# How the second token chunk's normalized input gets from token order to feature order through device memory

## The chip, the core and the metric

The kernel runs on one core of a Trainium2 chip. The metric is the device time of one launch in microseconds (us), taken as the median of several runs. The trace comes from one profiled execution of the same program. Five engines work side by side, each through its own list of instructions in order, and wait for one another through semaphores: TensorE (PE in the profile, with PEld for its weight loads), VectorE (DVE), ScalarE (ACT), GpSimd (POOL) and SyncE (SP). SP computes nothing; it issues all of this kernel's transfers between device memory and the on-chip memory, in the order of its list.

## What is computed

The input is 2048 tokens of 512 features, all in float32. After a first layernorm there are two branches: sliding-window attention with 32 heads of 16 and a window of 256, and a channel MLP with 1792 hidden units. Their product is added to the input:

```python
xn = _layernorm(x)
s = attention(xn, wqkv) @ wo            # 32 heads, causal, window 256
y = _layernorm(xn)
h = gelu(y @ w1 + b1)                   # 512 -> 1792
g = silu(h @ w2 + b2)                   # 1792 -> 512
return x + s * g
```

## The kernel before

**Stages.** The first 430 us or so are the attention with its projections, and the weights being brought in. What follows is the MLP, chunk by chunk of 512 tokens (c = 0 to 3). In chunks 0 and 1 the loop over `i` takes the 14 hidden blocks of 128 units one by one. A float32 product is made of three passes of halves: each operand is split into a rounded "high" part and the rest, the "low" part. So a hidden block is 12 matmuls (`hidden`), then ACT applies gelu with the bias (`activate`), ACT writes the high part `gh`, DVE the low part `gl` (`split_g`), and 12 matmuls (`project`) add the block into the four accumulators `acc` (tokens by features). At the end of a chunk `end_chunk` multiplies the attention outputs `ohl` with `wo` (matmuls into `s`, 48 in all), applies silu to `acc`, multiplies, adds x and stores.

**Two layouts.** The layernorm needs tokens on the partitions, the hidden matmul needs features on the partitions. For chunk 1, `y_steps` normalizes four tiles of 128 tokens by 512 features in `mlp["y"]` while chunk 0 is in its loop (i = 3 and 4). Then `turn_y(1, range(4))` transposes each tile on DVE, in place, in blocks of 32 by 32, and SP writes each tile to the scratch tensor `z_d` in device memory, 256 KB a tile, in rows of 2 KB. At i = 5 `fetch_y(1, kt, ...)` reads it back for the four feature blocks kt = 0 to 3: four transfers a block, 16 in all, each of 32 partitions with 16 pieces of 32 numbers (128 bytes), which puts the 32 by 32 blocks in their places. So `mlp["yy"][1][kt]` holds features by tokens. Last, `split` copies the high part into `mlp["yy"][0][kt]` on ACT and subtracts on DVE, at i = 12 for kt 0, at 13 for kt 1 and at 14 for kt 2 and 3. Chunks 2 and 3 use the same two functions later on.

**Attention outputs.** In the same loop `load_o(0, g)` brings in, for g = 0 to 3, the attention output `or` (from `oT_d`) and the inverse row sums into the end of the tile `w` (from `rden_d`, each row repeated for 16 partitions). `rden_d` is written by SP at i = 5, after DVE has made the reciprocals `den`, and the four pairs of loads follow it on SP's queue, then the 16 transfers of `fetch_y`. DVE multiplies pair g at i = 9 + g, and `split_o` splits the product at i = 10 + g.

**What sets the order.** Every engine's instructions are kept in program order here. On DVE the multiplication of pair 0 stands just ahead of `gl` of hidden block 10; on ACT the copy of feature block kt stands between the `gh` of one hidden block and the gelu of the next. The tile `g_first`, which has the same place in memory (tag `wa`) as the `gated` tile of `end_chunk`, holds the two hidden blocks that are used first. SP's list goes on, behind the `fetch_y` of chunk 1, with the four loads of the next y tiles and the four loads of x for `end_chunk`.

Hidden blocks run in the order 2, 3, 0, 1, 4, 5, 6 to 13 in chunk 0 and 0 to 13 in chunk 1. In the profile nearly every instruction has line L43, that of a helper through which they are all recorded, so groups are told apart by their tiles' names.

Of the kernel before, what the change touches and what calls it, by code (L numbers as in the profile page):

```python
# [9 lines left out]
F32 = mybir.dt.float32  # L10
F32R = mybir.dt.float32r
I32 = mybir.dt.int32
AF = mybir.ActivationFunctionType
# [4 lines left out]
S, D, H, DH, WIN, F = 2048, 512, 32, 16, 256, 1792  # L18
P = 128
NCH = S // 512  # L20
# [30 lines left out]
def mixer_kernel(ctx, tc, x, wqk, wv, wo, w1, b1, w2, b2, out):  # L51


    nc = SimpleNamespace(**{name: Ordered(tc, name) for name in ("tensor", "vector", "scalar", "gpsimd", "sync")})

    const = ctx.enter_context(tc.tile_pool(name="const", bufs=1))
    bigp = ctx.enter_context(tc.tile_pool(name="bigp", bufs=1))
    t2 = ctx.enter_context(tc.tile_pool(name="t2", bufs=5))
    small = ctx.enter_context(tc.tile_pool(name="small", bufs=3))
    dram = ctx.enter_context(tc.tile_pool(name="dram", bufs=1, space=bass.MemoryType.DRAM))  # L60
# [16 lines left out]
    def load(pool, tag, src, name, shape=(P, 512)):  # L77
        t = pool.tile(list(shape), F32, tag=tag, name=name)
        nc.sync.dma_start(t, src)
        return t  # L80
# [102 lines left out]
    oT_d = dram.tile([4, 8, 32, S], F32, name="oT_d")  # L183
# [2 lines left out]
    w_d = {"w1": dram.tile([P, NF * 512], F32, name="w1_d"), "w2": dram.tile([P, NF * 512], F32, name="w2_d"),  # L186
           "wo": dram.tile([P, 4 * 512], F32, name="wo_d")}
    g_d = dram.tile([NF, P, 512], F32, name="g_d")
    z_d = dram.tile([NCH - 1, 4, P, 512], F32, name="z_d")
    mT_d = dram.tile([NQ, NCH, 32, P], F32, name="mT_d")  # L190


# [45 lines left out]
    b1s = const.tile([P, NF], F32, name="b1s")  # L238
# [346 lines left out]
    mlp = {}  # L585
# [54 lines left out]
    def y_steps(a, b):  # L640
        run(mlp["ln"][a:b])

    def hidden_mm(ps, f, k):
        kt, (a, b) = k // 3, PASSES[k % 3]
        nc.tensor.matmul(ps, w1_part(a, f)[:, P * kt: P * (kt + 1)], mlp["yy"][b][kt],
                         start=(k == 0), stop=(k == 3 * KT - 1))
# [49 lines left out]
    n, raw = raws["qk"]  # L696
# [176 lines left out]
    for f in range(6, NF, 2):  # L873
        t = gp.tile([P, 2, 512], F32, tag="ohl", name=f"hr_{f}", bufs=4)
# [9 lines left out]
    def load_y(c):  # L884
        return load_x(c, ((mlp["yp"], "y"),), "y")

    def turn_y(c, tiles):

        for i in tiles:
            y = mlp["y"][i]  # L890
            nc.vector.transpose(y, y)
            nc.sync.dma_start(z_d[c - 1, i], y)

    def fetch_y(c, kt, dst):

        for k in range(4):
            at = z_d[c - 1, 0, 0, 128 * kt + 32 * k: 128 * kt + 32 * k + 32]
            nc.sync.dma_start(dst[32 * k: 32 * k + 32].rearrange("p (t j) -> p t j", j=32),
                              bass.AP(tensor=at.tensor, offset=at.offset, ap=[[512, 32], [32 * 512, 16], [1, 32]]))

    def load_o(c, g):

        cols = slice(512 * c, 512 * (c + 1))
        pool, tag = (t2, "t2") if c else (mlp["yp"], "y")
        raw = load(pool, tag, oT_d[g, :, 0:DH, cols], f"or_{c}_{g}")
        rec = mlp["w2", g // 2][:, 512 * (14 + g % 2): 512 * (15 + g % 2)].bitcast(F32)
        nc.sync.dma_start(rec, bass.AP(tensor=rden_d.tensor, offset=rden_d.offset + 8 * g * S + 512 * c,
                                       ap=[[S, 8], [0, DH], [1, 512]]))
        return raw, rec

    def split_o(c, g, raw):
        ohl = gp.tile([P, 2, 512], F32R, tag="ohl", name=f"ohl_{c}_{g}", bufs=4)
# [6 lines left out]
    def open_accs(c):  # L919
        return [ps_mx.tile([P, 2, 512], F32, tag="mx", name=f"acc_{c}_{i}") for i in range(2)]  # L920

    def split_g(c, f, g, cast):
        gh = gp.tile([P, 512], F32R, tag="gh", name=f"gh_{c}_{f}")
        gl = gp.tile([P, 512], F32R, tag="gl", name=f"gl_{c}_{f}")
        split(gh, gl, g, cast)
        return gh, gl
# [154 lines left out]
    for c in range(2):  # L1081
        accs = open_accs(c)
        gs, os_, hs, wanted = {}, [], {}, []
        made = ready if c == 0 else {}

        def hidden(f):
            hs[f] = (ps_yt if c and f % 2 else ps_st).tile([P, 512], F32, tag="b", name=f"h_{c}_{f}")
            for k in range(3 * KT):
                hidden_mm(hs[f], f, k)

        def activate(f):
            if f in made and f in soon:
                gs[f] = made[f]
                return
            src = made[f] if f in made else hs.pop(f)
            g = src if f in made and f < 2 else t2.tile([P, 512], F32, tag="t2", name=f"g_{c}_{f}")
            nc.scalar.activation(g, src, AF.Gelu_apprx_tanh, bias=b1s[:, f: f + 1])
            gs[f] = split_g(c, f, g, nc.scalar.copy)

        order = [2, 3, 0, 1, 4, 5, *range(6, NF)] if c == 0 else [*range(NF)]  # L1100
        ahead = 2 + c
        for f in range(ahead if c else 0):
            hidden(f)
        o_from, o_late = (0, 0) if c else (7, 1)
        nc.sync.on = True
        for i in range(NF + 1):
            if i < NF:
                activate(order[i])
            if c and i in (1, 2, 6, 7):
                y_steps(6, 10)  # L1110
            if c and i >= 10 and i < 14:
                second_y(i - 10)
            if c and i == 14:
                kept["w"] = bigp.tile([P, 768], F32R, tag="wb1", name="wsh")
                combine_w(0)
            if c == 0:
                for kind, f in late_w[LATE[i]: LATE[i + 1]]:
                    settle(kind, f, nc.scalar.copy, nc.vector)
            if i >= 1:
                project(accs, [(order[i - 1], gs.pop(order[i - 1]))], order[0], order[-1])  # L1120
            if i + ahead < NF and order[i + ahead] not in made and order[i + ahead] > 1:
                hidden(order[i + ahead])
            if c == 0:
                if i == 3:
                    mlp["ln"] = layernorm(mlp["y"], "C1", True)
                    y_steps(0, 5)
                if i == 4:
                    y_steps(5, 10)
                    turn_y(1, range(4))
                if i in (4, 5):  # L1130
                    for j in (2 * i - 8, 2 * i - 7):
                        nc.vector.reciprocal(den[:, P * j: P * (j + 1)], den[:, P * j: P * (j + 1)])
                if i == 5:
                    nc.sync.dma_start(rden_d.rearrange("g a (c t) -> (g a c) t", c=NCH), den)
                    wanted += [load_o(0, g) for g in range(4)]
                    for kt in range(KT):
                        fetch_y(1, kt, mlp["yy"][1][kt].bitcast(F32))
                for kt in {12: (0,), 13: (1,), 14: (2, 3)}.get(i, ()):
                    split(mlp["yy"][0][kt], mlp["yy"][1][kt], mlp["yy"][1][kt].bitcast(F32))
            else:  # L1140
                steps2(i)
            k = i - o_from
            if 0 <= k - 2 - o_late < 4:
                os_.append(split_o(c, k - 2 - o_late, wanted[k - 2 - o_late][0]))
            if 0 <= k - 1 - o_late < 4:
                nc.vector.tensor_mul(wanted[k - 1 - o_late][0], *wanted[k - 1 - o_late])
            if c and 0 <= k < 4:
                wanted.append(load_o(c, k))
            if c == 0 and i == NF:
                mlp["y"] = load_y(2)  # L1150
            if c:
                if i in (2, 3, 7, 8):
                    turn_y(2 + i // 5, (0, 1) if i in (2, 7) else (2, 3))
                if i == 3:
                    mlp["y"] = load_y(3)
                    kept[0] = gated[:, 2:4]
                    kept[1] = bigp.tile([P, 2, 512], F32, tag="wb1", name="y2_21")
                    for kt in range(KT):
                        fetch_y(2, kt, kept[kt // 2][:, kt % 2])
                if i in (8, 9):  # L1160
                    for kt in (2 * i - 16, 2 * i - 15):
                        put("21" if kt > 1 else "11", kt % 2, kept[kt // 2][:, kt % 2])
                if i == 8:
                    fetch_second()
                if i == 12:
                    fetch_pair(0)
            if c and i in (0, 1, 5, 6):
                y_steps(5, 6)
        nc.sync.on = False
        if c == 0:  # L1170
            gated = bigp.tile([P, 4, 512], F32, tag="wa", name="gated")

        def between(i):
            if c == 1 and i in (1, 2):
                split_w(0, 2 * i - 2)
                split_w(0, 2 * i - 1)
        end_chunk(c, accs, os_, between)
        if c == 0:
            steps2(-1)
# [99 lines left out]
    for i in range(NF):  # L1279
# [9 lines left out]
        if 5 <= i < 9:  # L1289
            raw, rec = wanted  # L1290
            nc.vector.tensor_mul(raw, raw, rec)
        if 4 <= i < 8:
            wanted = load_o(3, i - 4)
# [34 lines left out]
```

## Time and profile before

| | us |
|---|---|
| median of 3 runs | 747.17 |
| lowest and highest run | 746.42 and 747.22 |
| the profiled execution's own time | 746.98 |
| its span, first to last instruction | 745.2 |
| PE busy in the span | 728.8 (98%) |
| DVE busy | 516.5 (69%) |
| ACT busy | 440.1 (59%) |
| POOL busy | 297.5 (40%) |

How to read what is quoted below: a row of the timeline has start, length, engine, line, operation, tile written and tiles read, shapes, how often, and in brackets the idle time before it and what ended it. A row of the chain of waits has start, length, who held the chain, and how many instructions. Times count from the start of the span. `SPq` is SP's queue. A busy PE is one that has matmuls in its pipeline.

### The profile page before, as it was taken

The numbers are of one execution on the slowest core, as the hardware profiler recorded it, in microseconds if no ns is written. First come the engines' busy times: TensorE is split into PE (matmuls) and PEld (weight loads), VectorE is DVE, ScalarE is ACT, GpSimd is POOL, SyncE is SP. The second block draws the span as 40 slices with busy tenths as digits, with TensorE's granted clock in tenths as the row PEclk, the third lists the DMA queues.
The fourth block names the chain that finished last, engine by engine and source line by source line (L and its number), as shares of the span: only waits on it lengthen the run. The fifth ranks groups of instructions, "written<-read, shape, count | busy, mean of one in ns | idle before, by whom it ended". The sixth has DMA issues, their size and how long they took to land.

```text
span 745.2 us, 18812 instructions
## 1 busy us (share of the span) xinstructions
PE 728.8 (98%) x7360; PEld 585.6 (79%) x7360; DVE 516.5 (69%) x790; ACT 440.1 (59%) x744; POOL 297.5 (40%) x644
## 2 busy tenths in 40 slices
PE   8999999999999999999999999999999999999997
PEld 7886777777778887777776688788888888888886
DVE  6886777877766678887773567656658755676643
ACT  7757767867667676778877756443544734442001
POOL 7413757757666555767867700020102000001102
PEclk9999999999999999999999999999999999999999
DMA  8633355757555624646735385745453322253611
GB/s 289 192 71 77 86 137 149 210 151 194 142 133 153 154 71 149 163 129 165 201 103 161 92 286 201 198 143 194 110 108 113 96 88 74 69 181 117 214 55 56
DMA packets 84025, 105.71 MB, mean 142 GB/s; under 512 B 36640, under 2 KB 36896, under 8 KB 83936
## 3 DMA queue, kind: packets, MB, share of 16 engines
q1 hardware_dynamic: 83936, 104.50, 49.5%
q8 instruction: 58, 0.95, 0.5%
q14 instruction: 31, 0.25, 0.1%
HBM read 54.53 MB, written 32.77 MB: 117 GB/s over the span
## 4 chain that ended last, share of the span: by engine, by line
PE 86%; ACT 5%; DVE 3%; DMA 2%; issue 1%; POOL 1%; SPq 1%; DVEq 0%; ACTq 0%; POOLq 0%
PE fb L43 19%; PE acc L43 17%; PE zo L43 12%; PE stb L43 9%; PE p L43 9%; PE s L43 6%; PE h L43 6%; PE xy L43 5%; ACT pt L43 4%; PE pv L43 3%; POOL pt L43 1%; DVE xy L43 1%; SPq L43 1%; DMA w<-rden_d 1%; DMA xnT<-z_d 1%
## 5 line engine op out<-in xcount | busy, mean ns | idle before, releaser
L43 POOL TENSOR_SCALAR_AFFINE_SELECT pt<-pt 128x256 f32<-128x256 f32 x480 | 192.9, 425 | 133.7 <-ACT pt L43 131.7
L43 ACT ACTIVATE pt<-stb 128x768 f32<-128x768 f32 (+1 forms) x244 | 188.5, 773 | 62.4 <-PE stb L43 55.1
L43 DVE TENSOR_REDUCE mt<-xy 128x4 f32<-128x1024 f32 (+1 forms) x128 | 152.6, 1192 | 4.4
L43 DVE COPY_PREDICATED xy<-upper,zo 128x512 f32<-128x512 int32 x112 | 77.8, 695 | 70.6 <-PE xy L43 63.1
L43 POOL TENSOR_TENSOR xo<-xo,gated 128x512 f32<-128x512 f32 x15 | 19.9, 1330 | 236.9 <-DVE gated L43 195.5
L43 PE MATMUL fb<-xnT,wqb 64*128 64x512 f32 (+1 forms) x684 | 104.6, 397 | 0.2
L43 PE MATMUL zo<-pt,vt 128*17 128x128 f32 x2880 | 103.7, 275 | 0.3 <-POOL pt L43 0.3
L43 PE MATMUL stb<-qk 64*128 64x384 f32 (+1 forms) x488 | 97.1, 393 | 6.2 <-ACT pt L43 3.9
L43 PE MATMUL acc<-w,gh 128*128 128x512 f32 x320 | 98.6, 389 | 0.4 <-ACT gh L43 0.4
L43 PEld LDWEIGHTS stb<-qk 64*128 64x128 f32 x488 | 45.8, 183 | 51.5 <-ACT pt L43 46.3
L43 PEld LDWEIGHTS zo<-pt,vt 128*17 128x17 f32 x2880 | 67.5, 97 | 15.6 <-issue 6.3
L43 PEld LDWEIGHTS fb<-xnT,wqb 64*128 64x128 f32 (+1 forms) x684 | 64.7, 185 | 11.0 <-DVE pjr L43 1.4
L43 PEld LDWEIGHTS acc<-w,gh 128*128 128x128 f32 x320 | 60.0, 188 | 13.1 <-ACT gh L43 0.8
L43 PE MATMUL acc<-w,gl 128*128 128x512 f32 x160 | 62.3, 390 | 1.0 <-DVE gl L43 1.0
L43 PE MATMUL xy<-qk 64*128 64x256 f32 (+2 forms) x536 | 58.4, 291 | 0.2
L43 PEld LDWEIGHTS xy<-qk 64*128 64x128 f32 x536 | 46.6, 185 | 6.6 <-issue 3.1
L43 ACT COPY oraw<-zo 128x128 f32<-128x128 f32 x128 | 34.0, 266 | 29.4 <-PE zo L43 28.7
L43 PE MATMUL s<-wos,ohl 128*128 128x512 f32 (+1 forms) x204 | 44.3, 376 | 0.0
L43 ACT ACTIVATE gated<-acc 128x512 f32<-128x512 f32 x16 | 8.7, 596 | 59.3 <-DVE acc L43 59.3
L43 PEld LDWEIGHTS s<-wos,ohl 128*128 128x128 f32 x204 | 36.8, 188 | 7.1
L43 PEld LDWEIGHTS zo<-qk 64*128 64x128 f32 x448 | 38.5, 185 | 4.6 <-issue 1.4
L43 ACT COPY p<-p 128x512 f32<-128x512 f32 x21 | 12.3, 585 | 48.9 <-PE p L43 41.2
(191 smaller groups left out, 1233.8 us busy)
## 6 DMA issues: line engine op xcount, KB each, us to landing
qk<-sh SPq DMA_DIRECT2D x128, 128.0 KB
qk<-pjr SPq DMA_DIRECT2D x64, 128.0 KB
oT_d<-oraw SPq DMA_DIRECT2D x32, 256.0 KB
w_d<-in_w_dram SPq DMA_DIRECT2D x14, 512.0 KB
x<-in_x_dram SPq DMA_DIRECT2D x16, 256.0 KB
or<-oT_d SPq DMA_DIRECT2D x16, 256.0 KB
w<-rden_d SPq DMA_DIRECT2D x16, 256.0 KB
xo<-in_x_dram SPq DMA_DIRECT2D x16, 256.0 KB
```

What stands on the lines that cost most here:

```text
L43: r = issue(*args, **kwargs)
```

## The change

Chunk 1's y takes another way through memory, and some steps around it move.

- DVE transposes the four y tiles out of place into one tile `whole` (tag `wa`), so that the four token tiles' blocks of 32 lie next to one another: 128 numbers, 512 bytes, for each feature block of 32.
- SP writes `whole` to a new scratch tensor `zt_d` (features by tokens) in four transfers of 32 partitions by 16 pieces of 512 bytes, instead of four transfers in rows of 2 KB.
- SP reads each feature block back in one load of 128 rows of 2 KB, four in all, instead of 16 transfers of 128-byte pieces.
- The token columns come back in another order (32-token blocks of the four tiles interleaved). The 14 gelu instructions of chunk 1 write them back in order, through an output access pattern with runs of 32 numbers.
- `load_o` is cut in two. For chunk 0 the four `or` loads now stand ahead of the write of `rden_d`, and the four loads of the inverse sums behind the four loads of y.
- The split of feature block 0 moves from i = 12 to i = 9.
- `z_d` has one part less; chunks 2 and 3 use it as before.

```diff
-    z_d = dram.tile([NCH - 1, 4, P, 512], F32, name="z_d")
+    z_d = dram.tile([2, 4, P, 512], F32, name="z_d")
+    zt_d = dram.tile([S // 4, 512], F32, name="zt_d")
...
-            nc.sync.dma_start(z_d[c - 1, i], y)
+            nc.sync.dma_start(z_d[c - 2, i], y)
...
-    def load_o(c, g):
-
-        cols = slice(512 * c, 512 * (c + 1))
+    def load_raw(c, g):
+
         pool, tag = (t2, "t2") if c else (mlp["yp"], "y")
-        raw = load(pool, tag, oT_d[g, :, 0:DH, cols], f"or_{c}_{g}")
+        return load(pool, tag, oT_d[g, :, 0:DH, 512 * c: 512 * (c + 1)], f"or_{c}_{g}")
+
+    def load_rec(c, g):
+
         rec = mlp["w2", g // 2][:, 512 * (14 + g % 2): 512 * (15 + g % 2)].bitcast(F32)
         nc.sync.dma_start(rec, bass.AP(tensor=rden_d.tensor, offset=rden_d.offset + 8 * g * S + 512 * c,
                                        ap=[[S, 8], [0, DH], [1, 512]]))
-        return raw, rec
+        return rec
+
+    def load_o(c, g):
+        return load_raw(c, g), load_rec(c, g)
...
-            nc.scalar.activation(g, src, AF.Gelu_apprx_tanh, bias=b1s[:, f: f + 1])
+            to = g
+            if c:
+                src = src.rearrange("p (a i t) -> p a i t", a=4, i=4)
+                to = g.rearrange("p (i a t) -> p a i t", a=4, i=4)
+            nc.scalar.activation(to, src, AF.Gelu_apprx_tanh, bias=b1s[:, f: f + 1])
...
                 if i == 4:
                     y_steps(5, 10)
-                    turn_y(1, range(4))
+                    whole = bigp.tile([P, 16, 4, 32], F32, tag="wa", name="y_1")
+                    for j, y in enumerate(mlp["y"]):
+                        nc.vector.transpose(whole[:, :, j], y.rearrange("p (b t) -> p b t", t=32))
...
                 if i == 5:
+                    for a in range(4):
+                        nc.sync.dma_start(zt_d[:, P * a: P * (a + 1)].rearrange("(b p) t -> p b t", p=32),
+                                          whole[32 * a: 32 * a + 32].rearrange("p b i t -> p b (i t)"))
+                    first_o = [load_raw(0, g) for g in range(4)]
                     nc.sync.dma_start(rden_d.rearrange("g a (c t) -> (g a c) t", c=NCH), den)
-                    wanted += [load_o(0, g) for g in range(4)]
                     for kt in range(KT):
-                        fetch_y(1, kt, mlp["yy"][1][kt].bitcast(F32))
-                for kt in {12: (0,), 13: (1,), 14: (2, 3)}.get(i, ()):
+                        nc.sync.dma_start(mlp["yy"][1][kt].bitcast(F32), zt_d[P * kt: P * (kt + 1)])
+                    wanted += [(first_o[g], load_rec(0, g)) for g in range(4)]
+                for kt in {9: (0,), 13: (1,), 14: (2, 3)}.get(i, ()):
```

More of the change, by code (lines that the diff above doesn't have):

```diff
@@ L891, in turn_y @@
             nc.vector.transpose(y, y)
-            nc.sync.dma_start(z_d[c - 1, i], y)
+            nc.sync.dma_start(z_d[c - 2, i], y)
     def fetch_y(c, kt, dst):
         for k in range(4):
-            at = z_d[c - 1, 0, 0, 128 * kt + 32 * k: 128 * kt + 32 * k + 32]
+            at = z_d[c - 2, 0, 0, 128 * kt + 32 * k: 128 * kt + 32 * k + 32]
             nc.sync.dma_start(dst[32 * k: 32 * k + 32].rearrange("p (t j) -> p t j", j=32),
                               bass.AP(tensor=at.tensor, offset=at.offset, ap=[[512, 32], [32 * 512, 16], [1, 32]]))
-    def load_o(c, g):
-        cols = slice(512 * c, 512 * (c + 1))
+    def load_raw(c, g):
         pool, tag = (t2, "t2") if c else (mlp["yp"], "y")
-        raw = load(pool, tag, oT_d[g, :, 0:DH, cols], f"or_{c}_{g}")
+        return load(pool, tag, oT_d[g, :, 0:DH, 512 * c: 512 * (c + 1)], f"or_{c}_{g}")
+    def load_rec(c, g):
         rec = mlp["w2", g // 2][:, 512 * (14 + g % 2): 512 * (15 + g % 2)].bitcast(F32)
```

## The prediction, made before the changed kernel was run

> **What bounds the kernel now.** First the page: PE is busy in nearly all of the span. So only PE's idle time can be won, and I asked next whom PE waits for from 400 us on, which covers everything that the edit touches.
>
> ```profile
> PE 728.8 (98%) x7360; PEld 585.6 (79%) x7360; DVE 516.5 (69%) x790; ACT 440.1 (59%) x744; POOL 297.5 (40%) x644
> ...
> PE acc L43 <- DVE gl L43: 1.0, 1, 1.0
> PE acc L43 <- ACT gh L43: 0.4, 1, 0.4
> ```
>
> Two short waits, both in the projection of chunk 0's last hidden block. The chain of waits around them, in order of time:
>
> ```profile
> 446.32 5.07 PE acc L43 x23
> ...
> 453.69 1.98 DMA rden_d<-den
> ...
> 455.68 6.14 DMA w<-rden_d
> ...
> 461.84 1.96 SPq L43
> ...
> 463.85 3.41 SPq L43
> ...
> 467.30 4.53 DMA xnT<-z_d
> ...
> 475.60 2.56 PE acc L43 x10
> 478.16 10.88 PE s L43 x48
> ...
> 499.92 2.72 PE acc L43 x12
> ...
> 729.76 11.04 PE s L43 x60
> ```
>
> The chain leaves PE, goes through the inverse sums (`w`), SP's queue and the first small load of y, and comes back at 475.60. Twelve matmuls take 2.72. From 446.32 to the `s` matmuls stand eleven blocks of twelve (f = 1 and 4 to 13): 29.92, so `s` could start at 476.24. It starts at 478.16. **The stall is 1.92**, more than the 1.4 of the two waits, as PE also refills. After 478.16 the chain is PE to the end: one microsecond later there is one microsecond at the end, and nothing more can be won.
>
> Why the stall arises is read from ACT and DVE:
>
> ```profile
> 462.50 0.62 ACT L43 CAST gh<-g 128x512 fp32r<-128x512 f32 x1 [0.95 <-ACT g L43]
> 471.93 0.62 ACT L43 CAST yh<-xnT 128x512 fp32r<-128x512 f32 x1 [3.37 <-DMA xnT<-z_d]
> 473.21 0.62 ACT L43 CAST gh<-g 128x512 fp32r<-128x512 f32 x1
> 446.36 2.83 DVE L43 STREAM_TRANSPOSE y<-y 128x512 f32<-128x512 f32 x4 [0.89 <-ACT y L43]
> 450.76 0.63 DVE L43 TENSOR_TENSOR gl<-g,gh 128x512 fp32r<-128x512 f32 x1
> 453.58 0.63 DVE L43 TENSOR_TENSOR gl<-g,gh 128x512 fp32r<-128x512 f32 x1
> 461.91 0.69 DVE L43 TENSOR_TENSOR or<-or,w 128x512 f32<-128x512 f32 x1 [0.18 <-issue]
> 463.15 0.69 DVE L43 TENSOR_TENSOR gl<-g,gh 128x512 fp32r<-128x512 f32 x1 [0.55 <-ACT gh L43]
> 468.03 0.69 DVE L43 TENSOR_TENSOR or<-or,w 128x512 f32<-128x512 f32 x1 [0.40 <-DMA w<-rden_d]
> 474.26 0.68 DVE L43 TENSOR_TENSOR or<-or,w 128x512 f32<-128x512 f32 x1
> 474.86 0.69 DVE L43 TENSOR_TENSOR gl<-g,gh 128x512 fp32r<-128x512 f32 x1
> ```
>
> ACT's copy of y's block 0 waits for its transfers until 471.93; behind it stand the last hidden block's gelu and `gh` (473.21), and behind its subtraction on DVE `gl` (474.86). Their transfers are late because SP's queue holds the four `or` and four `w` loads first, and these are slow:
>
> ```profile
> 450.00:451.00 1.00, 1.00 (x6) 0.83 (x5) 1.00 (x3) 0.82 (x2) 0.00 (x0) 1.00 1.06 408
> 466.00:467.00 1.00, 1.00 (x6) 0.82 (x5) 0.97 (x3) 0.46 (x1) 0.00 (x0) 1.00 0.61 212
> 472.00:473.00 1.00, 1.00 (x6) 0.84 (x5) 0.41 (x1) 1.00 (x2) 0.00 (x0) 1.00 0.78 122
> ...
> 461.19 15.22 SPq L43 DMA_DIRECT2D xnT<-z_d  x16
> ```
>
> In the three windows the last two columns are the mean busy share of the 16 DMA engines and GB/s. Whole rows of 2 KB to and from 128 partitions (450) move 408 GB/s with all engines busy; the `or` and `w` loads (466) have about half of them, 212 GB/s; the 128-byte pieces (472) move 122, and SP needs 15.22 for issuing the 16 of them.
>
> [...]
>
> **The change, part by part.** *Removed:* 16 loads of 128-byte pieces, and with them the wait of 3.37 on ACT at block 13. That gives back the 1.92. *Gelu:* 14 instructions write in runs of 32 numbers. The nearest rows are copies with short runs (16 of 17 numbers, `vt`) beside contiguous ones, on both engines:
>
> ```profile
> L43 ACT COPY vt<-pv 128x512 f32<-128x512 f32 x8 | 4.6, 579 | 9.9 <-PE pv L43 9.9
> L43 ACT COPY pjr<-fb 128x512 f32<-128x512 f32 x15 | 8.8, 585 | 2.1 <-PE stb L43 1.0 <-PE fb L43 0.7
> L43 ACT ACTIVATE g<-h,b1s 128x512 f32<-128x512 f32 x16 | 10.9, 679 | 2.5 <-PE h L43 2.4
> L43 DVE COPY vt<-fb 128x512 f32<-128x512 f32 x4 | 2.7, 680 | 0.0
> L43 DVE COPY pjr<-fb 128x512 f32<-128x512 f32 x13 | 8.8, 680 | 0.0
> 499.90:554.30 54.40, 54.40 (x242) 45.05 (x241) 34.37 (x70) 26.54 (x43) 3.47 (x3) 1.00 0.55 145
> ```
>
> 579 against 585 ns: no price. Were a gelu twice as long, that is 14 x 0.68 = 9.5 us of ACT, hidden under PE: ACT is busy for 26.5 of chunk 1's 54.4. *Transposes:* 680 against 680 on DVE, so they stay at 2.83 together. Here the cover is thin: behind them stand `gl` of blocks 5 and 6, done at 451.39 and 454.21, and PE uses them here:
>
> ```profile
> 452.05 0.39 PE L43 MATMUL acc<-w,gl 128*128 128x512 f32 x1
> 454.77 0.39 PE L43 MATMUL acc<-w,gl 128*128 128x512 f32 x1
> 465.20 0.61 PE L43 MATMUL acc<-w,gh 128*128 128x512 f32 x2
> 465.65 0.39 PE L43 MATMUL acc<-w,gl 128*128 128x512 f32 x1
> ```
>
> The slack is 0.66 and 0.56: the four may cost 0.56 more, not more.
>
> *Moved, and this decides:* the inverse sums now stand behind everything else. Their first user, the product `or` x `w` of pair 0, precedes `gl` of block 10 on DVE. PE needs that `gl` at 465.65; before it go 0.60 for the product (474.26 to 474.86), 0.69 for `gl` and 0.05 for the semaphore. So **w 0 must have landed by 464.3**, and each microsecond later stalls PE as long. Later pairs have 2.72 more each, and need about 1.5 more; only pair 0 counts. Its landing, step by step on SP's queue:
>
> - The four writes of `zt_d` start when the transposes are done, 446.36 + 2.83 = 449.2. A write of 256 KB into a quiet queue takes 1.98 (`rden_d`); at 408 GB/s 0.64 of it is data, so 1.3 is latency.
> - Their 1.05 MB in 512-byte pieces are in no row. Between 408 GB/s (2.6 us) and 122 (8.6). One engine's time for a piece is 16 x 2048 B / 408 GB/s = 80 ns at 2 KB and 17 ns at 128 B; on the line between them 512 B takes 29.5 ns, 2048 pieces on 16 engines 3.8 us. I take it, as 122 is also held down by SP's issuing many small transfers. Landed: 454.3.
> - Four `or` loads, queued behind. From w 0's landing (455.68 + 6.14 = 461.82) to w 2's (468.03) four loads of the kind passed: 1.55 each, 6.2 together. 460.5.
> - `rden_d`, 0.64: 461.1. Only then can SP issue w 0; the four y loads, issued before at about 454, are in between, 0.64 each: y 0 at 461.8, the last at 463.7.
> - w 0, 1.55: **465.3**. That is 1.0 late.
>
> The wait of ACT for y's block 0, now at i = 9, has `gh` of block 10 behind it: copy, gelu and `gh` need 1.9, PE wants it at 465.2, so y 0 may land at 463.3; 461.8 is in time. Blocks 1 to 3 are split from 471 on, long landed. On SP the next y tiles and x wait behind the w loads instead of 16 small ones that ended at 476, so earlier than now.
>
> **Sum:** 746.98 - 1.92 + 1.0 = 746.06 for the profiled execution, which lies 0.19 under the median; on the median 747.17 - 0.92 = 746.25. Its own range, with w 0 between just in time and 6.14 after its issue at 461.1 (467.2, 2.9 late): 745.2 to 748.2.
>
> **Rivals.** *Full gain.* The 512-byte pieces move at the rate of whole rows: 1.2 less, w 0 at 464.1, no new stall, 745.25. For it: PE waits nowhere else. Against it: `or` and `w` have to keep to 1.55 each, and w 0 took 6.14 before.
>
> [...]
>
> *Slower: slow pieces.* At 122 GB/s the writes take 4.8 longer, and all that queues behind them with them: w 0 at 470.1, a new stall of 5.8, minus 1.92, so 751.1. It is slower than before once w 0 lands after 466.2, and by over 0.2% (1.5) after 467.7, that is with pieces below about 170 GB/s, 6.2 us. For it: the one small-piece row; against it: that row's share of 0.78 shows engines not full. *Slower: transposes.* If strided writing doubled their 2.83, PE would stall 2.3 at block 6 and, with w 0 moved along by 0.5 net, 1.5 at block 10: 747.17 - 1.92 + 3.8 = 749.0. Against it: the `vt` rows. *It doesn't do what it says* would be y landing late still, after 463.3; that falls with the slow pieces.
>
> **How the numbers follow.** The forecast (some of the gain given back, inside 0.2%) 0.48; full gain 0.33; slow pieces 0.13; transposes 0.06. A measurement here tells about 0.2%, 1.5 us, from no change, so faster is the full gain, 0.33; the same 0.48; slower 0.19. The range takes in the full gain with half a microsecond of scatter, and above the forecast's own 748.2 the near part of the slower cases: 744.8 to 748.9.
>
> **What would show it.** Right: no DMA wait on ACT at block 13; the only PE wait from 430 on is at block 10, released by DVE, which waits for `w<-rden_d`, about a microsecond; `s` starts near 477.2. Full gain: no PE wait, `s` at 476.2. Wrong: a DMA share below 0.6 while `zt_d` is written, ACT waiting for y at block 9, transposes longer than 0.85 each, or gelu far above 0.68.

## The result, and the profile after

| | before | after |
|---|---|---|
| median of 6 runs each, us | 747.06 | 750.28 |
| lowest and highest run | 746.42 and 747.22 | 749.77 and 751.03 |
| profiled execution's own time | 746.98 | 750.31 |
| its span | 745.2 | 748.6 |

The ratio is 1.0045, with a 95% interval of 1.0032 to 1.0058: the change makes the kernel slower by 3.2 us. The forecast was 0.9 faster, and the result lies 1.4 above the upper end of the range.

The first thing to look at is the page's first line, busy time and share of the span by engine:

```profile
PE 730.9 (98%) x7360; PEld 587.0 (78%) x7360; DVE 517.0 (69%) x790; ACT 439.9 (59%) x744; POOL 297.6 (40%) x644
```

Then the waits of PE from 400 us on (total, times, longest):

```profile
PE acc L43 <- DVE gl L43: 2.0, 1, 2.0
PE acc L43 <- ACT gh L43: 0.8, 1, 0.8
```

PE still waits twice, for 2.8 instead of 1.4. And it is *busy* 2.1 longer, 730.9 against 728.8, with the same 7360 matmuls. So something made the matmuls themselves slower. The chain of waits (start, length, holder, instructions) shows where:

```profile
446.46 6.45 PE acc L43 x29
...
455.79 7.90 DMA rden_d<-den
463.75 3.76 DMA w<-rden_d
...
468.22 0.69 DVE gl L43
468.96 12.37 PE acc L43 x46
481.33 10.88 PE s L43 x48
```

The chain now runs through `rden_d` and `w`, ends in `gl` of hidden block 10, and goes on at 468.96 with the 46 matmuls that are left before `s`. These 46 take 12.37; at 2.72 for twelve they would take 10.43. `s` starts at 481.33 instead of 478.16, 3.2 later, which is the loss.

SP's timeline (start, time that SP was held, transfers) has the landing step by step:

```profile
449.36 2.95 SPq L43 DMA_DIRECT2D zt_d<-y  x4
452.40 3.29 SPq L43 DMA_DIRECT2D or<-oT_d  x4
455.79 0.67 SPq L43 DMA_DIRECT2D rden_d<-den  x1
...
463.75 2.47 SPq L43 DMA_DIRECT2D w<-rden_d  x4
```

Issuing the four writes and the four `or` loads holds SP until 455.7, so the write of `rden_d` is issued at 455.79. It lands 7.90 later, at 463.69; only then can SP issue `w`, and w 0 lands 3.76 after that, at 467.5. On ACT and DVE this becomes:

```profile
464.31 0.62 ACT L43 CAST yh<-xnT 128x512 fp32r<-128x512 f32 x1 [3.26 <-DMA xnT<-zt_d]
...
465.59 0.62 ACT L43 CAST gh<-g 128x512 fp32r<-128x512 f32 x1
...
467.61 0.69 DVE L43 TENSOR_TENSOR or<-or,w 128x512 f32<-128x512 f32 x1 [1.96 <-DMA w<-rden_d]
468.22 0.68 DVE L43 TENSOR_TENSOR gl<-g,gh 128x512 fp32r<-128x512 f32 x1
```

ACT waits for y's block 0 until 464.31, which makes `gh` of block 10 late. DVE waits for w 0 until 467.61, which makes `gl` of block 10 later still. PE's timeline (idle time before a row in brackets):

```profile
466.26 0.73 PE L43 MATMUL acc<-w,gh 128*128 128x512 f32 x2 [0.76 <-ACT gh L43]
468.96 0.51 PE L43 MATMUL acc<-w,gl 128*128 128x512 f32 x1 [1.97 <-DVE gl L43]
...
471.15 1.06 PE L43 MATMUL acc<-w,gh 128*128 128x512 f32 x2
...
476.41 0.62 PE L43 MATMUL acc<-w,gh 128*128 128x512 f32 x2
```

The same pair of matmuls takes 1.06 at 471.15 and 0.62 at 476.41. The windows say why (busy time of PE, PEld, DVE, ACT, POOL, then PE's granted clock, share of the DMA engines, GB/s):

```profile
465.00:469.00 4.00, 1.27 (x6) 0.41 (x4) 2.04 (x4) 3.04 (x5) 0.00 (x0) 1.00 0.49 165
469.00:470.00 1.00, 1.00 (x5) 0.82 (x5) 0.97 (x3) 0.00 (x0) 0.00 (x0) 1.00 0.52 166
470.00:474.00 4.00, 4.00 (x12) 3.16 (x11) 3.84 (x7) 1.24 (x2) 0.00 (x0) 0.57 0.71 215
474.00:478.00 4.00, 4.00 (x20) 3.26 (x19) 2.90 (x5) 2.24 (x5) 0.00 (x0) 1.00 0.92 313
```

From 465 to 469 PE works only 1.27 of 4.00. A microsecond after it has started again, the granted clock falls: 0.57 on the mean from 470 to 474, and 1.00 again after that. Twelve matmuls fit into the four microseconds at the low clock, 20 into the next four.

So the account is: the old stall is gone, -1.92. PE takes up `gl` of block 10 at 468.96; before it did so at 465.65, and this execution runs 0.14 later from 446 on (446.46 against 446.32), so the new stall is 3.2. The slow matmuls cost 12.37 - 10.43 = 1.9. Together 3.2, with the 0.14 some 3.3; `s` starts 3.2 later.

### The profile page after: what moved, and what is told of

The parts are those of the page before. It is cut to its first block, busy times and chain, and to the rows that moved or that the text cites. A ratio compares the mean times of both kernels' runs of the same rounds, so it can differ in the third digit from the quotient of the medians.

```text
span 748.6 us, 18773 instructions
## 1 busy us (share of the span) xinstructions
PE 730.9 (98%) x7360; PEld 587.0 (78%) x7360; DVE 517.0 (69%) x790; ACT 439.9 (59%) x744; POOL 297.6 (40%) x644
## 4 chain that ended last, share of the span: by engine, by line
PE 85%; ACT 4%; DMA 4%; DVE 3%; issue 2%; POOL 1%; SPq 0%; DVEq 0%; ACTq 0%; POOLq 0%
PE acc L43 19%; PE fb L43 18%; PE zo L43 11%; PE p L43 9%; PE stb L43 8%; PE s L43 6%; PE h L43 6%; PE xy L43 5%; ACT pt L43 4%; PE pv L43 3%; DMA qk<-qk 2%; POOL pt L43 1%; DMA rden_d<-den 1%; DVE xy L43 1%; DMA x<-in_x_dram 1%
```

## The experiments

The theory had three parts. **T1**: the loss comes from w 0's late landing, and that from the loads of `or` on the queue ahead of it (1a: the queue of transfers itself is slow; its rival 1b: SP's wait for `rden_d` is what holds `w`). Another rival says that the split of y's block 0, moved to i = 9, causes it by its wait on ACT. **T2**: what comes on top of the stall is the clock, which falls because PE was idle. **T3**, formed after numbers 1 to 4: what makes this queue slow is that `or` and `w`, with an outermost dimension of 8, run on half of the DMA engines. In the profile before, the window in which they are under way (466 to 467) has a DMA share of 0.61, that of whole rows of 2 KB (450 to 451) 1.06. In the expectations, "the eight rings" stands for the half of the DMA engines that this theory supposes for `or` and `w`; no run shows how a single engine takes its transfers. Diffs are against the changed kernel unless they say otherwise; each time stands beside runs of the kernel before on the same chip, whose medians are 746.79 (for 1 to 4), 746.69 (5 and 6) and 746.84 (7 to 9).

**1. The early split.** Block 0 is split at i = 12, as before.

```diff
-                for kt in {9: (0,), 13: (1,), 14: (2, 3)}.get(i, ()):
+                for kt in {12: (0,), 13: (1,), 14: (2, 3)}.get(i, ()):
```

> The changed kernel with the split of y's block 0 back at i = 12; all else as changed. Theory 1 (the inverse sums w 0 land late and hold gl of block 10 on DVE): nothing changes, w 0 still lands near 467.5, PE still waits about 3 us at block 10, 750.3 within 0.5. Rival (the early split is what stalls: ACT waits for y until 464.3 with gh of block 10 behind it): the stall goes, 745 to 747.

Measured 750.04, ratio 1.0046 (1.0034 to 1.0058). The waits of PE in this run, and then its chain:

```profile
PE acc L43 <- DVE gl L43: 2.9, 1, 2.9
```

The chain:

```profile
463.06 3.80 DMA w<-rden_d
...
468.30 12.32 PE acc L43 x46
480.62 10.88 PE s L43 x48
```

The wait for `gh` is gone, and the one for `gl` takes it over: 2.9 instead of 0.8 + 2.0. The slow 46 matmuls stay. The rival falls; ACT's wait for y was hidden behind the one for w 0.

**2. SP's wait.** `rden_d` is written ahead of the `or` loads, so that it has long landed when SP comes to `w`.

```diff
-                    first_o = [load_raw(0, g) for g in range(4)]
                     nc.sync.dma_start(rden_d.rearrange("g a (c t) -> (g a c) t", c=NCH), den)
+                    first_o = [load_raw(0, g) for g in range(4)]
```

> The changed kernel with the write of rden_d ahead of the four or loads on SP's queue; the w loads stay behind y. Theory 1a (the eight rings work in order, so w 0 stays behind four or and four y loads however early SP can issue it): w 0 lands at 466 to 467.5, 748 to 750.3. Theory 1b (SP's wait for the landing of rden_d, 463.7, is what delays w 0): w 0 is issued by 459, lands 3.8 later before 464, no stall, 745.2.

Measured 751.12, ratio 1.0057 (1.0045 to 1.0069). Chain of this run:

```profile
458.72 9.28 DMA w<-rden_d
...
469.37 13.57 PE acc L43 x46
482.94 10.88 PE s L43 x48
```

`w` is issued 5.0 earlier, at 458.72 instead of 463.75, and lands at 468.0, not a bit earlier than 467.5. So SP's wait isn't what makes w 0 late: it is late in the queue, behind `or` and y (1a). Landing and time are a little above what was expected of 1a, 467.5 and 750.3; the 46 matmuls take 1.2 longer than in the changed kernel, as the clock is at 0.50 for all six microseconds from 469 to 475, where the changed kernel has it at 0.50 for 3.41 (last section).

**3. and 4. Another order on the queue.** Two pairs of `or` and `w` ahead of y and two behind (3), or all four pairs ahead of y as before the change (4); in both `rden_d` comes first and the split of block 0 stands at i = 12. The edit of 3 and, for 4, the same with all pairs in the first place:

```diff
-                    first_o = [load_raw(0, g) for g in range(4)]
                     nc.sync.dma_start(rden_d.rearrange("g a (c t) -> (g a c) t", c=NCH), den)
+                    wanted += [load_o(0, g) for g in range(2)]
                     for kt in range(KT):
                         nc.sync.dma_start(mlp["yy"][1][kt].bitcast(F32), zt_d[P * kt: P * (kt + 1)])
-                    wanted += [(first_o[g], load_rec(0, g)) for g in range(4)]
+                    wanted += [load_o(0, g) for g in range(2, 4)]
```

> The changed kernel with the order on SP: zt_d, rden_d, or 0, w 0, or 1, w 1, the four y loads, or 2, w 2, or 3, w 3; split of block 0 at i = 12. Theory 1: w 0 lands near 461.5 and y by 467, nobody is late, PE waits nowhere from 430 on and the whole 1.9 of the old stall is won: 745.2. Rival (the new way of y through memory costs something by itself, in the transposes, the 512-byte writes or the gelu): above 747.

> The new way of y through memory in the old order: zt_d, rden_d, the four pairs or and w, then the four y loads; split of block 0 at i = 12. Theory 1: y waits on the eight rings behind w 3 and lands at 471.5 to 473, so ACT stalls at block 13 as before the change and nothing is won: 747 to 748. Rival (the 16 small transfers were what made y late): y lands before 468, 745.2.

Number 3 measured 751.35 with a wide scatter (747.53 to 752.78), ratio 1.0056 (1.0037 to 1.0075). That expectation failed: y and the first two products come nearly in time, but DVE waits for w 2, and PE for it. The timelines of DVE and PE:

```profile
474.58 0.69 DVE L43 TENSOR_TENSOR or<-or,w 128x512 f32<-128x512 f32 x1 [4.98 <-DMA w<-rden_d]
...
475.93 0.79 PE L43 MATMUL acc<-w,gl 128*128 128x512 f32 x1 [4.32 <-DVE gl L43]
```

The window behind has the clock at 0.50 for six microseconds:

```profile
474.00:480.00 6.00, 4.07 (x10) 3.21 (x11) 5.36 (x10) 0.49 (x1) 0.00 (x0) 0.50 0.39 133
```

So far whatever was put last on this queue came too late: w 2 lands at 474.5 here.

Number 4 measured 749.12 (748.46 to 752.5), ratio 1.0042 (1.0027 to 1.0058), some 1 to 2 above what was expected. ACT's timeline:

```profile
473.89 0.62 ACT L43 CAST yh<-xnT 128x512 fp32r<-128x512 f32 x1 [5.83 <-DMA xnT<-zt_d]
```

This is the kernel before with nothing but y's new way, and y 0 lands at 473.9, *later* than the 471.9 of the 16 loads in 128-byte pieces. So the small pieces that the change does away with were not what made y late. The trace also records each rise of a transfer's semaphore: fifteen of y 0's sixteen records stand by 471.4, the last one comes 2.5 later. Why that one lags isn't shown.

**5. The clock.** Ten matmuls whose result nobody reads fill PE's idle time ahead of the projection of block 10.

```diff
+            if c == 0 and i == 11:
+                idle = ps_yt.tile([P, 512], F32, tag="b", name="idle")
+                for _ in range(10):
+                    nc.tensor.matmul(idle, w2_part(0, 9)[:, 0:P], w2_part(0, 9), start=True, stop=True)
```

> The changed kernel with ten more matmuls of 0.227 us into an unused bank ahead of the projection of block 10; their result is not used. Theory 2 (PE's idle time at block 10 halves its clock for 3.4 us and that costs 1.9 of the loss): they fill 2.3 of the stall, the granted clock stays at 1.0 there, and the kernel with 2.3 us more of work is about 1.9 faster than the changed one, 748.4. Rival (the clock drop has another cause, or costs nothing): 750.3 or more.

Measured 748.29, ratio 1.0021 (1.0012 to 1.0030). PE's timeline:

```profile
465.25 2.43 PE L43 MATMUL idle<-w 128*128 128x512 f32 x10
...
468.81 0.50 PE L43 MATMUL acc<-w,gl 128*128 128x512 f32 x1 [0.67 <-DVE gl L43]
```

The window in which the clock had fallen:

```profile
470.00:474.00 4.00, 4.00 (x19) 3.29 (x19) 3.93 (x8) 1.31 (x3) 0.00 (x0) 1.00 0.54 148
```

And the chain behind the stall:

```profile
468.81 10.72 PE acc L43 x46
```

PE takes up `gl` as late as in the changed kernel (468.81 and 468.96), but the clock stays at 1.00, 19 matmuls instead of 12 fit from 470 to 474, and the 46 take 10.72 instead of 12.37. The delay of `gl` is the same, so the 1.7 is the clock's: T2 holds.

**6. Another layout for `or` and `w`.** For chunk 0 both are read as 128 whole rows of 2 KB, the same number of bytes from other places; the attention outputs of chunk 0 are thus not those of the reference.

```diff
+        if c == 0:
+            rows = oT_d.rearrange("g a d t -> (g a d) t")[256 * g: 256 * g + P, 0:512]
+            return load(pool, tag, rows, f"or_{c}_{g}")
...
+        if c == 0:
+            nc.sync.dma_start(rec, rden_d.rearrange("g a (c t) -> (g a c) t", c=NCH))
+            return rec
```

> The changed kernel with the or and w loads of chunk 0 reading 128 whole rows in order (the same bytes, but other rows, so the attention outputs of chunk 0 are not the reference's). Theory 3 (the outermost dimension of 8 keeps these loads on half of the DMA engines, which everything else then queues behind): each of the eight loads takes about 0.7 instead of 1.5 to 2, w 0 lands before 463, no stall, 745.2. Rival (the loads are slow for their memory rows or for what runs beside them): w 0 still lands after 465, 748 or more.

Measured 745.24, ratio 0.9981 (0.9971 to 0.9990). The timelines of SP and DVE:

```profile
460.44 1.75 SPq L43 DMA_DIRECT2D w<-rden_d  x4
...
463.98 0.69 DVE L43 TENSOR_TENSOR or<-or,w 128x512 f32<-128x512 f32 x1 [1.63 <-DMA w<-rden_d]
```

The chain:

```profile
445.95 30.10 PE acc L43 x132
476.05 10.88 PE s L43 x48
```

`w` is issued 3.3 earlier, as `rden_d` lands earlier, and w 0 lands at 464.0, just in time though a microsecond later than expected. The DMA share from 456 to 464 is 0.98, at 323 GB/s; in the changed kernel it was 0.83, at 235 GB/s, from 454 to 464. PE runs its 132 matmuls through without a wait. Against the 746.69 beside it the gain is 1.5 of the 1.92 that could be won, and it comes from how two kinds of transfers are laid out; that 745.24 meets the prediction's full gain, 745.25, is in part chance, as that was worked out from 747.17.

The semaphore records of the traces say more. In the changed kernel a load of `or` or `w` has nine, one about a microsecond after its issue and eight as it lands; a transfer of `zt_d` or y has sixteen, and in number 6 so have `or` and `w`. In the changed kernel the write of `rden_d`, issued at 455.79, has eight of its sixteen by 458.1, and the other eight from 462.0 to 463.7, while the last `or` is done at 463.3. If each record stands for one DMA engine, which is the author's reading and not shown by itself, eight engines were free for it and eight were held up behind `or`. On that reading T3 holds, for `or` and `w` together.

**7. to 9. The inverse sums with an outermost dimension of 16.** `rden_d` is kept twice in memory, so that the load of `w` has an outermost dimension of 16 and not 8. Here nothing is left out of the computation. In the table, "`w` on 16" stands for that layout. The edit goes into number 4 (7), into the kernel before (8) and into the changed kernel (9):

```diff
-    rden_d = dram.tile([4, 8, S], F32, name="rden_d")
+    rden_d = dram.tile([4, 8, 2, S], F32, name="rden_d")
...
-        nc.sync.dma_start(rec, bass.AP(tensor=rden_d.tensor, offset=rden_d.offset + 8 * g * S + 512 * c,
-                                       ap=[[S, 8], [0, DH], [1, 512]]))
+        nc.sync.dma_start(rec, bass.AP(tensor=rden_d.tensor, offset=rden_d.offset + 16 * g * S + 512 * c,
+                                       ap=[[S, 16], [0, DH // 2], [1, 512]]))
...
-                    nc.sync.dma_start(rden_d.rearrange("g a (c t) -> (g a c) t", c=NCH), den)
+                    for two in range(2):
+                        nc.sync.dma_start(rden_d[:, :, two].rearrange("g a (c t) -> g a c t", c=NCH), den)
```

> The new way of y through memory in the old order (zt_d, rden_d, the four pairs, y; split of block 0 at i = 12), with rden_d kept twice in memory so that the w loads have an outermost dimension of 16. Theory 3 (half of the DMA engines): the w loads take about 0.7 instead of 1.5, w 0 lands near 460, w 3 near 467 and y by 469.5, in time for everyone; no PE wait from 430 on, 745.0 to 745.4. Rival (an outermost dimension of 16 changes nothing): 749, as the same order without it.

> The kernel before, with rden_d kept twice so that the w loads have an outermost dimension of 16; y goes its old way, in 16 transfers of 128-byte pieces. Theory 3: what made y late before the change were the loads on half of the engines ahead of it, not its small pieces; y 0 lands at 467 to 469, the stall goes without the change, 745.0 to 745.6. Rival (the 16 small transfers are slow by themselves): the stall stays, 746.5 to 747.

> The changed kernel, order untouched, with rden_d kept twice and the w loads on an outermost dimension of 16. Theory 1 (w 0 is gated by the landing of rden_d behind the four or loads): rden_d still lands after 463.5, w 0 is issued then and lands at 466.5 to 467.5, the stall at block 10 stays above 2 us and 748.5 to 750.3 is measured. Rival (w 0's own slow load is the delay): below 747.

| | median, us | ratio to before (95%) |
|---|---|---|
| 7: pairs first, y's new way, `w` on 16 | 746.87 | 1.0001 (0.9990 to 1.0012) |
| 8: the kernel before, `w` on 16 | 745.41 | 0.9983 (0.9974 to 0.9992) |
| 9: the changed kernel, `w` on 16 | 751.12 | 1.0054 (1.0042 to 1.0067) |

Number 8, ACT's timeline:

```profile
469.58 0.62 ACT L43 CAST yh<-xnT 128x512 fp32r<-128x512 f32 x1 [1.39 <-DMA xnT<-z_d]
```

Its chain:

```profile
445.95 29.92 PE acc L43 x132
475.87 10.88 PE s L43 x48
```

y 0, in its old 128-byte pieces, lands at 469.5 instead of 471.9, and PE has no wait left. Number 8 beats both kernels: it is 1.4 faster than the kernel before, and keeps y's old way through memory. Number 7 differs from it in y's way, new instead of old, and is slower; ACT's row of it:

```profile
470.98 0.62 ACT L43 CAST yh<-xnT 128x512 fp32r<-128x512 f32 x1 [2.64 <-DMA xnT<-zt_d]
```

y 0 is 1.4 later than in number 8, and PE waits 0.9 for it; why the new way is slower here isn't shown. The expected 745.0 to 745.4 was missed, but against number 4 the wider `w` brought 2.2. Number 9, the chain:

```profile
456.32 8.19 DMA rden_d<-den
464.58 3.76 DMA w<-rden_d
...
469.79 12.34 PE acc L43 x46
```

In the changed order a wider `w` alone is of no use: `rden_d` still needs 8.19 behind the `or` loads, whose outermost dimension stays 8, and SP waits for it. w 0 lands at 468.3 and the time is 751.12, both 0.8 above the upper end of what was expected.

In numbers 6 and 8 the loads with the new layout have sixteen semaphore records instead of nine, and what stands behind them lands earlier: w 0 at 464.0 instead of 467.5 in number 6, y 0 at 469.5 instead of 471.9 in number 8. From 452 to 464 number 8 has a DMA share of 0.52, at 174 GB/s, and the kernel before 0.41, at 134 GB/s.

## Why the prediction was wrong, point by point

- *The old stall of 1.92 can be won back.* Right: ACT has no wait at block 13 any more, and number 6, without a new stall, gains 1.5 (745.24 against 746.69).
- *Gelu costs nothing, the transposes stay at 2.83.* Right; grouped by shape, gelu takes 678 ns on the mean of 16, against 679:

```profile
L43 ACT ACTIVATE g<-h,b1s 128x512 f32<-128x512 f32 x16 | 10.9, 678 | 2.5 <-PE h L43 2.4
```

  DVE's timeline has the four transposes at 2.83:

```profile
446.50 2.83 DVE L43 STREAM_TRANSPOSE y<-y 128x512 f32<-128x512 f32 x4 [0.89 <-ACT y L43]
```

- *The new stall sits at block 10, in `gl`, behind the product that waits for w 0.* Right in place and cause; the second wait at block 10, for `gh`, was not foreseen, but number 1 shows that it costs nothing by itself.
- *w 0 lands at 465.3.* Wrong, it was 467.5, and this is the first term that was mis-sized. By the semaphore records the four writes of `zt_d` took 6.2 from the first issue to the last landing, at 455.6, where the sum had 5.1; and the four `or` loads behind them were done at 463.3, 7.8 later and not 6.2. So `rden_d`, half of it held up behind `or`, landed at 463.7, against 461.1 in the sum. The last part was no longer than thought: w 0 came 3.8 after its issue, where the sum had 4.2 with y in between. The stall is 3.2 instead of 1.0. The upper end of the forecast's own range, 467.2, nearly covered this. That what comes later on the queue waits behind `or` and `w` was an assumption of the sum; number 2 showed it for `w`, which was issued 5.0 earlier and landed no earlier, and the records of `rden_d` show it for half of that write. The full-gain rival's term, 512-byte pieces at the rate of whole rows, is shown by no run; in a window of the changed kernel they moved at 219 GB/s, against 408 (last section).
- *y 0 at 461.8 is in time.* Wrong: 464.3, a microsecond behind the deadline of 463.3. The steps ahead of it are the same as for w 0.
- *"Each microsecond later stalls PE as long."* This is the step that failed in kind. With PE idle 0.76 + 1.97 within 3.5 us the granted clock fell to 0.50, for 3.41 us, and the stall of 3.2 cost 5.1. Number 5 shows the 1.7 to 1.9 of it to be the clock's. By stall alone the time would have been some 748.3, near what number 5 measured and inside the range; no rival had a clock in it, though the profile has a column for it. The slow-pieces rival came near in its time, 751.1, by another mechanism: its w 0 is at 470.1.

The clock records of the profile after have the granted clock full for 464.21 us, half for 3.41 and full again for 273.07; the kernel before has it full for 740.69 on end. The windows of the 3.41 us before the fall and of the 3.41 us at half, in the changed kernel (PE busy 1.44 of the first 3.41, so 1.97 idle):

```profile
466.72:470.13 3.41, 1.44 (x7) 0.99 (x6) 2.48 (x5) 1.35 (x3) 0.00 (x0) 1.00 0.48 163
470.13:473.54 3.41, 3.41 (x10) 2.66 (x9) 3.28 (x6) 1.24 (x2) 0.00 (x0) 0.50 0.75 227
```

Other profiled executions, by PE's idle time at its waits: 2.9 in number 1 was followed by a clock of 0.50 from 469 to 470, 1.5 and 2.2 in number 2 by 0.50 from 469 to 475, and 4.32 in number 3 goes with 0.50 from 474 to 480. The idle times of 0.4 and 1.0 in the kernel before left the clock at 1.00 (473 to 476), 0.67 in number 5 left it at 1.00 (470 to 474), and with 1.41 and 0.99 in number 4 the mean clock of the execution is 0.999 and the pair of matmuls behind them, at 477.89, takes 0.63. So the clock fell with 2.73 in two waits in the changed kernel, and not with 2.40 in two in number 4; what decides between them isn't shown.

The mean clock differs between the runs of one kernel: the changed kernel's six runs have 0.996 to 0.998, most runs of the kernel before 0.999 or 1.000, with a run of 749.15 at 0.997 among them. Those single runs have no trace, so why they differ isn't shown. Open is also what `or` alone in another layout would bring; number 9 shows that `w` alone brings nothing in the changed order.

## What to carry to other kernels

When a load is late on a queue, look first at what stands ahead of it, and at the windows' DMA share: here two kinds of transfers with an outermost dimension of 8 stood ahead, at a DMA share of 0.61 in the profile before, and a change of one layout (number 8, 745.41) did what a new way for the late load could not. Putting the late load ahead of the others only handed the delay to whatever stood last (w 2 at 474.5 in number 3, y 0 at 473.9 in number 4); give every transfer that is moved back its own deadline, with the wait of the in-order issuing engine for the write before it. And price a stall of TensorE with its clock: here 2.7 us of idle time close together brought more than half of the stall's length on top of it.

## What the runs showed of the hardware

- In the changed kernel the clock fell to 0.50 for 3.41 us, after 3.41 us in which PE was idle for 1.97. In numbers 2 and 3 it stayed there longer: the windows of both show 0.50 for six whole microseconds, with PE idle for another 0.37 of them in number 2 and 1.93 in number 3. Number 3's mean of 0.69 from 470 to 481 makes some 6.8 us at 0.50 (an estimate that takes the rest as full):

```profile
469.00:475.00 6.00, 5.63 (x13) 4.46 (x14) 4.87 (x10) 1.24 (x2) 0.00 (x0) 0.50 0.61 194
```

That is number 2, in which the 46 matmuls took 13.57. Number 3's six runs go from 747.53 at a mean clock of 0.999 to 752.78 at 0.995.

- Four writes in 512-byte pieces hold SP 2.95 (1.05 MB), and while nothing else is queued behind them yet, a window of the changed kernel shows 219 GB/s at a DMA share of 0.86, against 408 at 1.06 for whole rows of 2 KB (each of these writes also reads 32 partitions and not 128, and no run separates the two):

```profile
451.00:452.00 1.00, 1.00 (x6) 0.81 (x6) 1.00 (x2) 0.24 (x1) 0.00 (x0) 1.00 0.86 219
```
